# A depthwise convolution that takes taps two to seven over all channels at once, with x laid out as channels 3r+k, in a fused convolution and SiLU layer

## The chip, the core and the metric

The kernel runs on one core of a Trainium2 chip. The core has a matrix engine (TensorE), a vector engine (VectorE), a scalar engine (ScalarE), GpSimd, and SyncE, which here issues the transfers (DMAs). Each engine runs its own instructions in their order and waits on semaphores for the others. The metric is the device time of one execution in microseconds (us), less being better. Three runs of the kernel before took 2359.43, 2358.92 and 2358.91 us, median 2358.92.

## The reference

x has 8 sequences of 4096 tokens with 192 channels. A causal convolution over 7 tokens is followed by a two-layer network with SiLU, on 32768 tokens:

```python
w = np.exp(weight - np.max(weight, axis=-1, keepdims=True))
w = w / (np.sum(w, axis=-1, keepdims=True) + 1e-09)      # weight: (8 heads, 7 taps)
out = np.einsum('hk,bskhg->bshg', w, x_unf)               # head = 24 adjacent channels, same 7 taps
h = x @ w_in                                              # (32768, 192) @ (192, 2048)
g = h * (1.0 / (1.0 + np.exp(-h)))
return (g @ w_out).astype(np.float32)                     # (2048, 192)
```

All 24 channels of a head share their seven taps.

## The kernel before

**Tiling.** The tokens are worked through in 32 blocks of 1024. A block is two halves of 512 tokens. Channels lie in partitions: 64 of the 192 channels in 64 partitions, once for each half of the block, so that 128 partitions hold a third (k = 0, 1, 2) of the channels of all 1024 tokens, 512 elements long. In the kernel before, third k is channels 64k to 64k+63. x comes in with 12 transfers per block (`load`, L171), in runs of 32 channels (128 bytes), tokens in partitions; VectorE turns 32 x 32 pieces round (`turn_in`, L461, one instruction per third), the last six tokens of the half before are put in front (`halo_in`), and then `conv` (L489) does tap one on ScalarE and taps two to seven on VectorE, a multiply-and-add each, separately for each third: 3 + 18 instructions. The result is copied by 11 transfers (`spread`, L505) into the tile `dup`, for both row halves of TensorE, and `win` (L519) makes five sums and differences of it.

**The two matmuls.** Both use bilinear schemes that save products. Going up, sums of weight blocks (made once, by GpSimd) are multiplied with `win` or `dup`: 15 products (`product`, L611) for each of five groups, each 64 x 128 weights against 512 columns, on the upper or the lower row half of TensorE; two of them run side by side. A float32 matmul is two passes in the profile. A group's products go into three PSUM banks in chains: a product is added to a bank, the bank is read, the next product is added to the same bank. Which bank it is stands in `CHAIN_BANKS`; six more matmuls per block (`plain`, L635) use `PLAIN_BANKS`. Between products, ScalarE copies a bank out (`u`, L674), VectorE adds it to another bank (`X`, `a`, `b`, L668), and ScalarE takes SiLU (`S` L686, `SL` L691) into the tiles `g`. Going down, VectorE makes four differences `t` of `g` tiles for each of four j (`sum_g`, L694; three buffers `t`, shared with the output tile), and `out_slot` (L711, L741) multiplies: 48 slots per block of four matmuls side by side with 32 columns of weights each, into six banks. `merge` (L782) adds these up (M, y, x, z), `turn_out` transposes back and `store_out` writes.

**The order.** It is written out by hand in two lists and pinned. `START` opens the first blocks; `PLAN`, 129 slots divided by `|`, is run once per block. Slots are numbered from 0 here. A token names a step: P9.4 is product 9 of group 4; L.nk a plain matmul; u, X, a, b, S with a group after the point; t.ji difference i of j; Di.je a down slot; w.i a step of `win`; ld a load; i.k a transposition; v.ki tap i of third k (i from 0); sp.k a spread; o and st output. A `-` ahead means the block before, `+` the block after, and so i, v, sp and w work one block further ahead than the P beside them. Every engine gets its own part of the list in this order. In the list before, P and L stand in slots 50 to 128 and in 0 and 1, D in slots 2 to 49.

**The opening.** The softmax of the taps is spread to partitions by one matmul with a 0/1 matrix `hot` (L448); block 0's convolution is done on TensorE for two thirds, with diagonal matrices (L1001 to L1017), and its up and down products are plain. Meanwhile VectorE rounds the weights (`rounded`, L283).

Of the kernel before, what the change touches and what calls it, by code (L numbers as in the profile page):

```python
# [9 lines left out]
F32 = mybir.dt.float32  # L10
# [7 lines left out]
def kernel(  # L18
# [45 lines left out]
    assert D == NK * R == H * grp and NK == NP == 3 and S % TT == 0 and DFF == 4 * P * NJ  # L64
# [17 lines left out]
        "P5.0 | -P8.3 -S3.2 -sp.2 v.00 -t.01 | -D1.31 -S2.3 -S5.2 | -D1.01 -a0.2 -S1.3 =st.2 "  # L82
        "-a0.3 -S1.1 | -D1.11 -b5.3 -S0.2 | -D0.00 -S5.4 v.22 -sp.0 -S4.3 | -D2.01 -t.03 "
        "-S5.1 -S1.2 | -D0.20 =st.0 -t.02 -S0.3 | -D1.21 -S5.3 v.01 | -D2.00 v.11 | -D5.01 "
        "+ld.0 | -D0.30 v.02 | -D3.00 -t.10 | -D0.01 +ld.1 v.23 | -D0.31 v.24 | -D4.00 -t.11 "
        "+ld.2 | -D3.01 -w.0 | -D4.01 | -D0.11 -t.13 | -D2.11 -w.1 | -D5.00 | -D4.11 -t.12 | "
        "-D5.11 | -D2.10 -t.20 | -D4.10 -t.21 | -D5.10 | -D0.21 | -D0.10 -t.23 | -D3.11 "
        "-z1.0 v.25 u5.0 | -D4.20 v.03 | -D1.10 -t.22 | -D3.10 | -D4.21 -t.30 | -D1.20 v.12 "
        "| -D2.20 -t.31 | -D2.21 | -D1.30 -t.32 | -D3.21 -t.33 | -D5.20 | -D2.31 v.04 | "
        "-D1.00 v.26 | -D4.31 -w.2 | -D2.30 v.05 | -D5.30 -y2.0 | -D3.20 v.06 -y1.0 -M1.0 | "  # L90
        "-D3.31 v.13 | -D3.30 -M2.0 | -D5.31 v.14 -x0.0 | -D4.30 -y0.0 -M3.0 | -D5.21 -x1.0 "
        "| P2.0 | L.00 -M4.0 -x2.1 -w.3 | L.01 | P5.4 u4.0 -w.4 | L.02 | P6.0 u5.4 v.15 | "
        "P3.0 | P2.4 SL.0 v.16 u2.0 | L.12 -x2.3 X2.0 | L.11 -x2.2 u4.4 | L.10 -M5.0 | P9.0 "
        "| P1.0 +i.0 SL.2 SL.1 | P13.0 | P6.4 +i.1 -x2.0 u0.0 X4.0 | P3.4 | P5.1 u2.4 +i.2 "
        "S2.0 | P7.0 | P0.0 -M6.0 +ha.0 X2.4 | P12.0 | P11.0 u1.0 a5.0 u5.1 | P9.4 | P1.4 "
        "b1.0 S4.0 | P13.4 | P4.0 u0.4 X4.4 -w.5 | P10.0 | P2.1 a1.0 | P0.4 | P7.4 u4.1 b5.0 "
        "S2.4 | P11.4 | P8.0 -o.1 u1.4 a5.4 | P6.1 | P12.4 S4.4 a0.0 | P14.4 | P14.0 -M7.0 "
        "u2.1 S0.0 b1.4 | P4.4 | P3.1 S3.4 +v.10 | P10.4 | P1.1 X2.1 S3.0 a1.4 | P5.2 | P9.1 "
        "u0.1 | P0.1 | P13.1 u5.2 X4.1 | P2.2 b5.4 | P8.4 -o.3 | P7.1 | P5.3 u4.2 a0.4 -st.3 "
        "u1.1 | P6.2 | P12.1 S2.1 a5.1 u5.3 | P11.1 | P3.2 -st.1 b1.1 u2.2 S5.0 | P4.1 | "  # L100
        "P10.1 X2.2 S4.1 sp.1 | P2.3 S1.0 | P9.2 a1.1 -o.0 | P1.2 | P8.1 u4.3 X4.2 | P6.3 | "
        "P13.2 u0.2 a0.1 +v.20 | P11.2 b5.1 | P7.2 u2.3 -o.2 S2.2 | P0.2 | P3.3 S4.2 a5.2 | "
        "P1.3 | P12.2 u1.2 X2.3 | P4.2 u0.3 | P9.3 b1.2 S0.4 | P14.1 | P10.2 S1.4 X4.3 | "
        "P0.3 S3.1 | P7.3 b5.2 | P11.3 u1.3 a1.2 | P12.3 S0.1 a5.3 | P14.3 | P13.3 +v.21 | "
        "P4.3 S3.3 b1.3 | P8.2 a1.3 | P10.3 | P14.2 t.00"
# [1005 lines left out]
```

## Time and profile before

| | us |
|---|---|
| median of three runs | 2358.92 |
| the profiled execution | 2359.21 |
| its span, first to last instruction | 2357.4 |
| TensorE busy | 2349.2 |
| VectorE busy | 2110.6 |
| ScalarE busy | 1179.4 |
| taps two to seven, L498 (564 of 128x512, mean 755 ns) | 415.4 |
| transpositions of x, L464 (96 of 128x512, mean 687 ns) | 63.7 |

The page has the busy time of each engine; as instructions of one engine overlap a little, the busy time of a group can be more than the time it holds the engine up. A matmul of 512 columns is shown with 0.59 us, from its issue to the end of its results, while the next one on the same part of the array follows earlier. The timeline lists instructions by start, each with its length; a bracket is the idle time before it and what ended it. The chain is the sequence of work that ended last, followed back from the end. The granted TensorE clock was 0.999.

### The profile page before, as it was taken

How to read it: one execution, taken by the hardware profiler on the slowest of the kernel's cores; microseconds unless marked ns; L12 is line 12 of the kernel's file. 1: busy time of each engine (PE TensorE's matmuls, PEld its weight loads, DVE VectorE, ACT ScalarE, POOL GpSimd, SP SyncE). 2: the span in 40 equal slices, each digit the busy share in tenths (PEclk: the TensorE clock that was granted, in tenths of full speed). 3: DMA queues.
4: the chain of work that ended last, by engine and by line, in shares of the span. 5: the costliest groups of instructions: out<-in, count | busy, mean ns of one | idle time of the engine just before them, and what ended most of it. 6: DMA issues, size and time to landing. Idle time of an engine off the chain costs nothing.

```text
span 2357.4 us, 43991 instructions
## 1 busy us (share of the span) xinstructions
PE 2349.2 (100%) x17630; PEld 1043.8 (44%) x17630; DVE 2110.6 (90%) x2877; ACT 1179.4 (50%) x2275; POOL 105.7 (4%) x168
## 2 busy tenths in 40 slices
PE   9999999999999999999999999999999999999998
PEld 4344443444444444444444444444444444444444
DVE  8999989899899999998998999999999989899867
ACT  5345644456544465444564445654446644456443
POOL 4910000000000000000000000000000000000000
PEclk9999999999999999999999999999999999999999
DMA  7232111222112221222221122212222112222111
GB/s 158 51 66 52 37 35 35 52 53 47 26 33 52 53 53 29 38 40 52 53 43 28 35 53 52 52 23 36 48 52 52 36 32 37 52 53 39 21 20 28
DMA packets 451245, 106.56 MB, mean 45 GB/s; under 512 B 423584, under 2 KB 428704, under 8 KB 451040
## 3 DMA queue, kind: packets, MB, share of 16 engines
q1 hardware_dynamic: 447392, 101.78, 23.7%
q8 instruction: 138, 2.26, 0.4%
q0 software_dynamic: 448, 1.58, 0.3%
q10 hardware_dynamic: 3200, 0.39, 0.1%
q14 instruction: 67, 0.55, 0.1%
HBM read 31.46 MB, written 25.17 MB: 24 GB/s over the span
## 4 chain that ended last, share of the span: by engine, by line
PE 99%; DVE 1%; ACT 0%; issue 0%; ACTq 0%; DVEq 0%
PE ps L741 47%; PE ps L625 45%; PE ps L642 2%; PE ps L762 2%; PE ps L570 2%; PE ps L1010 1%; PE ps L422 0%; DVE t L709 0%; DVE g L668 0%; DVE cmb L819 0%; DVE cmb L162 0%; ACT u L162 0%; ACT yx L804 0%; DVE osb L162 0%; DVE win L532 0%
## 5 line engine op out<-in xcount | busy, mean ns | idle before, releaser
L741 PE MATMUL ps<-g,wo 128*32 128x512 f32 x2976 | 691.9, 592 | 0.0
L625 PE MATMUL ps<-win,wr 64*128 64x512 f32 x1550 | 691.3, 595 | 0.0
L625 PE MATMUL ps<-win,ws 64*128 64x512 f32 x1550 | 674.3, 603 | 0.6 <-ACT u L674 0.6
L674 ACT COPY u<-ps 128x512 f32<-128x512 f32 x775 | 445.8, 589 | 184.6 <-PE ps L625 158.0
L741 PE MATMUL ps<-t,wo 128*32 128x512 f32 (+2 forms) x4528 | 536.6, 446 | 0.5 <-DVE t L709 0.5
L741 PE MATMUL ps<-t,wx 128*32 128x512 f32 x2976 | 495.7, 592 | 0.0
L625 PE MATMUL ps<-dup,wr 64*128 64x512 f32 x868 | 423.8, 590 | 0.0
L498 DVE SCALAR_TENSOR_TENSOR nat<-xt,taps,nat 128x512 f32<-128x512 f32 x564 | 415.4, 755 | 5.6 <-ACT nat L495 2.0
L709 DVE TENSOR_TENSOR t<-g 128x1024 f32<-128x1024 f32 x248 | 299.9, 1220 | 61.1 <-PE ps L741 41.0
L709 DVE TENSOR_TENSOR t<-g,t 128x1024 f32<-128x1024 f32 x248 | 302.7, 1221 | 30.0 <-PE ps L741 24.7
L625 PEld LDWEIGHTS ps<-win,wr 64*128 64x128 f32 x1550 | 261.4, 186 | 148.3 <-issue 62.4
L686 ACT ACTIVATE g<-ps 128x512 f32<-128x512 f32 x465 | 275.4, 602 | 83.8 <-PE ps L625 78.0
L668 DVE TENSOR_TENSOR g<-u,ps 128x512 f32<-128x512 f32 x465 | 305.7, 673 | 10.1 <-PE ps L625 1.4
L741 PEld LDWEIGHTS ps<-t,wo 128*32 128x32 f32 x4528 | 185.4, 110 | 274.2 <-issue 270.6
L625 PEld LDWEIGHTS ps<-win,ws 64*128 64x128 f32 x1550 | 242.6, 185 | 144.8 <-issue 49.5
L625 PE MATMUL ps<-dup,ws 64*128 64x512 f32 x682 | 280.9, 602 | 0.0
L668 DVE TENSOR_TENSOR ps<-u,ps 128x512 f32<-128x512 f32 x310 | 214.5, 692 | 69.8 <-PE ps L625 64.0
L686 ACT ACTIVATE g<-g 128x512 f32<-128x512 f32 x465 | 268.4, 633 | 15.3 <-DVE g L668 15.3
L804 ACT COPY yx<-ps 32x512 f32<-32x512 f32 x150 | 84.2, 579 | 380.0 <-PE ps L741 377.6
L741 PE MATMUL ps<-g,wx 128*32 128x512 f32 x1488 | 246.0, 594 | 0.0
L741 PEld LDWEIGHTS ps<-g,wo 128*32 128x32 f32 x2976 | 170.1, 110 | 112.5 <-issue 103.9
L807 ACT COPY cmb<-ps 96x512 f32<-96x512 f32 x30 | 17.5, 583 | 403.8 <-PE ps L741 403.8
(90 smaller groups left out, 1849.2 us busy)
## 6 DMA issues: line engine op xcount, KB each, us to landing
dup<-nat SPq DMA_DIRECT2D x345, 128.0 KB, 2.3
nat<-in_x_dram SPq DMA_DIRECT2D x382, 64.0 KB, 2.4
out_dram<-osb SPq DMA_DIRECT2D x376, 64.0 KB, 2.0
raw<-in_moe_w_out_dram SPq DMA_DIRECT2D x8, 384.0 KB, 3.6
raw<-in_moe_w_in_dram SPq DMA_DIRECT2D x12, 192.0 KB, 4.5
ws<-wr POOLq DMA_DIRECT2D x8, 192.0 KB, 5.0
raw<-in_moe_w_in_dram SPq DMA_DIRECT2D x6, 128.0 KB, 3.0
xt<-xt SPq DMA_DIRECT2D x31, 4.5 KB, 1.9
```

The costliest lines, as they stand in the source:

```text
L498: nc.vector.scalar_tensor_tensor(out=dst, in0=src, scalar=tap, in1=dst, op0=ALU.mult, op1=ALU.add)
L570: nc.tensor.matmul(hs[a, n, e], rows(wr[j], e)[:, a, k, :], rows(d, e)[:, n, k, :], start=k == 0, stop=k == NK - 1,)
L625: nc.tensor.matmul(to[:, cols], raw(g, *LEFT[e][r], e), rhs[:, cols], start=first, stop=True, skip_group_check=True,)
L642: nc.tensor.matmul(banks[PLAIN_BANKS[n and 1 + e]][:, cols], rows(wr[j] if own == e else ws[j], e)[:, a, k, :], rows(dups[b], e)[:, SLOT[e ...
L668: pin(nc.vector.tensor_tensor(out_, u, v, op=op))
L674: pin(nc.scalar.copy(us[b, g, o][:, cols], t1[:, cols]))
L686: pin(nc.scalar.activation(h, src, AF.Silu))
L709: pin(nc.vector.tensor_tensor(t[i // 2][:, i % 2, :], u, v, op=ALU.subtract))
L741: nc.tensor.matmul(accs[b][at][SQ * q : SQ * q + SQ, to], lhs[:, e, SQ * k : SQ * k + SQ], rhs[:, e, ts(q, TB // 4) if i == 5 else to], st ...
L762: nc.tensor.matmul(banks[DOWN_BANKS[k]][R * n : R * n + R, :], wo[j][:, a, e, R * k : R * k + R], gs[b, j, a][:, n, e, :], start=j == 0 an ...
L804: pin(nc.scalar.copy(to, acc[3 * (name[0] == "x") + k][n:P, :]))
L1010: nc.tensor.matmul(by_pe[k][n], rows(diag, n)[:, k, i, :], rows(xts[0], n)[:, k, i : i + TB], start=i == 0, stop=i == K - 1,)
```

## The change

Third k becomes the channels 3r+k, in partition r. A head's 24 channels are then eight partitions in every third, so a partition has the same seven taps in all three thirds; `taps` shrinks from three columns per tap to one, and the matrix that spreads them from 96 rows to 8. Taps two to seven become one VectorE operation each over 128 x 3 x 512 elements (v.31 to v.36; the first tap stays with ScalarE, three operations). x is loaded in runs of 96 channels (384 bytes) with four transfers per block; the transposition of third k reads every third element of the token's row. The rows of w_in are taken as (r k). In the opening, block 0's x is loaded whole ahead of the first transposition, and one set of seven diagonal matrices replaces two. `PLAIN_BANKS` is (7, 4, 3) instead of (7, 7, 3). Both lists are new: in `PLAN` ten D slots (119 to 128) now stand between the last products and P5.0, -P8.3 of the next turn, which are followed by the other 38 (2 to 39); P and L stand in 40 to 118. The list `START` is left out below.

```diff
     PLAN = (
-        "P5.0 | -P8.3 -S3.2 -sp.2 v.00 -t.01 | -D1.31 -S2.3 -S5.2 | -D1.01 -a0.2 -S1.3 =st.2 "
-        "-a0.3 -S1.1 | -D1.11 -b5.3 -S0.2 | -D0.00 -S5.4 v.22 -sp.0 -S4.3 | -D2.01 -t.03 "
-        "-S5.1 -S1.2 | -D0.20 =st.0 -t.02 -S0.3 | -D1.21 -S5.3 v.01 | -D2.00 v.11 | -D5.01 "
-        "+ld.0 | -D0.30 v.02 | -D3.00 -t.10 | -D0.01 +ld.1 v.23 | -D0.31 v.24 | -D4.00 -t.11 "
-        "+ld.2 | -D3.01 -w.0 | -D4.01 | -D0.11 -t.13 | -D2.11 -w.1 | -D5.00 | -D4.11 -t.12 | "
-        "-D5.11 | -D2.10 -t.20 | -D4.10 -t.21 | -D5.10 | -D0.21 | -D0.10 -t.23 | -D3.11 "
-        "-z1.0 v.25 u5.0 | -D4.20 v.03 | -D1.10 -t.22 | -D3.10 | -D4.21 -t.30 | -D1.20 v.12 "
-        "| -D2.20 -t.31 | -D2.21 | -D1.30 -t.32 | -D3.21 -t.33 | -D5.20 | -D2.31 v.04 | "
-        "-D1.00 v.26 | -D4.31 -w.2 | -D2.30 v.05 | -D5.30 -y2.0 | -D3.20 v.06 -y1.0 -M1.0 | "
-        "-D3.31 v.13 | -D3.30 -M2.0 | -D5.31 v.14 -x0.0 | -D4.30 -y0.0 -M3.0 | -D5.21 -x1.0 "
-        "| P2.0 | L.00 -M4.0 -x2.1 -w.3 | L.01 | P5.4 u4.0 -w.4 | L.02 | P6.0 u5.4 v.15 | "
-        "P3.0 | P2.4 SL.0 v.16 u2.0 | L.12 -x2.3 X2.0 | L.11 -x2.2 u4.4 | L.10 -M5.0 | P9.0 "
-        "| P1.0 +i.0 SL.2 SL.1 | P13.0 | P6.4 +i.1 -x2.0 u0.0 X4.0 | P3.4 | P5.1 u2.4 +i.2 "
-        "S2.0 | P7.0 | P0.0 -M6.0 +ha.0 X2.4 | P12.0 | P11.0 u1.0 a5.0 u5.1 | P9.4 | P1.4 "
-        "b1.0 S4.0 | P13.4 | P4.0 u0.4 X4.4 -w.5 | P10.0 | P2.1 a1.0 | P0.4 | P7.4 u4.1 b5.0 "
-        "S2.4 | P11.4 | P8.0 -o.1 u1.4 a5.4 | P6.1 | P12.4 S4.4 a0.0 | P14.4 | P14.0 -M7.0 "
-        "u2.1 S0.0 b1.4 | P4.4 | P3.1 S3.4 +v.10 | P10.4 | P1.1 X2.1 S3.0 a1.4 | P5.2 | P9.1 "
-        "u0.1 | P0.1 | P13.1 u5.2 X4.1 | P2.2 b5.4 | P8.4 -o.3 | P7.1 | P5.3 u4.2 a0.4 -st.3 "
-        "u1.1 | P6.2 | P12.1 S2.1 a5.1 u5.3 | P11.1 | P3.2 -st.1 b1.1 u2.2 S5.0 | P4.1 | "
-        "P10.1 X2.2 S4.1 sp.1 | P2.3 S1.0 | P9.2 a1.1 -o.0 | P1.2 | P8.1 u4.3 X4.2 | P6.3 | "
-        "P13.2 u0.2 a0.1 +v.20 | P11.2 b5.1 | P7.2 u2.3 -o.2 S2.2 | P0.2 | P3.3 S4.2 a5.2 | "
-        "P1.3 | P12.2 u1.2 X2.3 | P4.2 u0.3 | P9.3 b1.2 S0.4 | P14.1 | P10.2 S1.4 X4.3 | "
-        "P0.3 S3.1 | P7.3 b5.2 | P11.3 u1.3 a1.2 | P12.3 S0.1 a5.3 | P14.3 | P13.3 +v.21 | "
-        "P4.3 S3.3 b1.3 | P8.2 a1.3 | P10.3 | P14.2 t.00"
+        "+ld.0 P5.0 | -P8.3 +ld.1 | -D2.10 -t.13 | -D3.01 -w.0 | -D5.01 | -D4.11 -t.20 | "
+        "-D2.11 -t.21 | -D1.31 | -D4.10 -w.1 | -D0.20 -t.23 | -D5.11 | -D2.21 -a0.3 | -D5.10 "
+        "v.32 -S0.3 | -D3.10 | -D1.01 -t.22 | -D3.11 | -D0.21 v.33 | -D2.20 | -D0.30 -t.30 | "
+        "-D4.21 -t.31 | -D3.20 | -D4.20 v.34 | -D0.01 | -D1.30 -w.2 | -D0.31 v.35 | -D2.30 | "
+        "-D2.31 -w.3 | -D3.21 -t.33 | -D0.11 -t.32 | -D1.00 -z1.0 -y2.0 v.36 | -D5.20 | "
+        "-D4.31 -y0.0 u5.0 | -D1.21 -w.5 | -D5.31 | -D5.30 | -D3.30 -M1.0 -w.4 | -D4.30 | "
+        "-D5.21 | -D3.31 -x2.1 -x2.0 | -D1.10 -x2.3 -M3.0 -x0.0 -x2.2 -M2.0 -y1.0 | L.00 | "
+        "P2.0 -x1.0 +i.0 | L.10 u4.0 +i.1 | P3.0 | P5.4 -M4.0 | L.01 | P6.0 u5.4 +i.2 | L.11 "
+        "u2.0 | L.02 | P2.4 X2.0 | L.12 -o.1 u4.4 | P9.0 | P1.0 SL.0 -M5.0 -st.1 SL.2 | P6.4 "
+        "| P13.0 u0.0 X4.0 SL.1 | P5.1 | P3.4 u2.4 S2.0 | P0.0 | P7.0 X2.4 | P11.0 | P12.0 "
+        "u1.0 a5.0 u5.1 | P1.4 | P9.4 b1.0 S4.0 | P4.0 | P13.4 u0.4 X4.4 | P10.0 | P2.1 a1.0 "
+        "| P0.4 | P7.4 b5.0 u4.1 | P11.4 | P8.0 u1.4 a5.4 S2.4 -M7.0 | P6.1 | P12.4 S1.0 "
+        "a0.0 | P4.4 | P14.4 u2.1 b1.4 | P3.1 | P14.0 S3.4 a1.4 S4.4 -o.2 | P1.1 | P10.4 "
+        "S5.0 X2.1 -st.2 | P5.2 | P8.4 u0.1 b5.4 | P9.1 | P0.1 a0.4 u5.2 +ha.0 S3.0 | P12.1 "
+        "| P2.2 X4.1 u1.1 -M6.0 | P13.1 | P5.3 u4.2 b1.1 | P7.1 | P6.2 S2.1 -o.0 | P3.2 "
+        "-st.0 | P11.1 a5.1 u2.2 | P10.1 u5.3 | P4.1 X2.2 S0.0 S4.1 | P9.2 | P1.2 b5.1 +v.00 "
+        "a1.1 | P13.2 | P2.3 u0.2 X4.2 S5.1 | P8.1 t.00 | P0.2 S2.2 u4.3 | P7.2 | P11.2 a0.1 "
+        "+v.10 | P12.2 u1.2 | P6.3 a5.2 S1.4 | P3.3 | P14.2 b1.2 u2.3 S4.2 | P10.2 X2.3 | "
+        "P1.3 | P9.3 | P4.2 b5.2 u0.3 | P0.3 | P12.3 X4.3 a1.2 | P11.3 | P7.3 u1.3 -o.3 S3.2 "
+        "| P13.3 | P14.1 b1.3 -st.3 S1.2 a5.3 S0.1 | P8.2 | P14.3 S4.3 t.02 | P4.3 | P10.3 "
+        "sp.1 S3.1 S5.2 t.01 | D0.00 S5.4 S0.4 | D1.20 b5.3 +v.20 sp.0 t.03 S2.3 | D1.11 "
+        "S1.1 | D0.10 a0.2 sp.2 t.10 | D5.00 | D3.00 a1.3 | D2.01 t.11 S1.3 | D4.01 S3.3 "
+        "S0.2 | D2.00 +v.31 S5.3 | D4.00 t.12"
     )
...
     START = (
...
     CHAIN_BANKS = ((0, 1, 7, 1, 0), (2, 3, 2, 3, 2), (4, 4, 4, 4, 4))
+    PLAIN_BANKS = (7, 4, 3)
...
-    def load(b, ks=range(NK)):
+    def load(b, ns=range(2)):
         if b not in nats:
-            nats[b] = nats[b % 2] if b > 1 else xpool.tile([P, NK, TB // SQ, SQ], F32, tag="nat", name="nat", bufs=2)
-        nat = nats[b]
-        for k in ks:
-            for i in range(P // SQ):
-                c = R * k + SQ * (i % 2)
-                queue = nc.scalar if not b and k == 0 and i % 2 == 0 else nc.sync
+            nats[b] = nats[b % 2] if b > 1 else xpool.tile([P, NK, TB], F32, tag="nat", name="nat", bufs=2)
+        flat = nats[b].rearrange("p k t -> p (k t)").rearrange("p (q d) -> p q d", d=HD)
+        for n in ns:
+            for e in range(2):
+                i = 2 * n + e
+                queue = nc.scalar if not b and not e else nc.sync
                 pin(
                     queue.dma_start(
-                        out=nat[SQ * i : SQ * i + SQ, k, :, :],
-                        in_=x_v[2 * b + i // 2][:, :, c : c + SQ],
+                        out=flat[SQ * i : SQ * i + SQ],
+                        in_=x_v[2 * b + n][:, :, HD * e : HD * e + HD],
                     )
                 )
 
...
-    x0 = x.flatten_outer_dims()[TB - pad : TB, :].rearrange("t (k c) -> c k t", k=NK)
+    x0 = x.flatten_outer_dims()[TB - pad : TB, :].rearrange("t (c k) -> c k t", k=NK)
...
-    hot = const.tile([KR, 2, R], F32, name="hot")
-    wown = const.tile([KR, NK, K], F32, name="wown")
+    hot = const.tile([H, 2, R], F32, name="hot")
+    wown = const.tile([H, K], F32, name="wown")
...
+    own = grp // NK
+    for sign, base in ((1, 0), (-1, own - 1)):
+        pool.affine_select(
+            out=hot,
+            in_=hot,
+            compare_op=ALU.is_ge,
+            fill=0.0,
+            base=base,
+            pattern=[[0, 2], [sign, R]],
+            channel_multiplier=-sign * own,
+        )
...
-    in32 = moe_w_in.bitcast(I32).rearrange("(k r) (a m c) -> r k a m c", r=R, a=2, m=NM)
+    in32 = moe_w_in.bitcast(I32).rearrange("(r k) (a m c) -> r k a m c", r=R, a=2, m=NM)
...
-    taps = const.tile([P, NK, K], F32, name="taps")
+    taps = const.tile([P, K], F32, name="taps")
...
-    load(0, (1, 2))
...
-    for k in range(NK):
-
-        vec.tensor_scalar(
-            wown[SQ * k : SQ * k + H, k, :], wexp, scalar1=part_, scalar2=None, op0=ALU.mult
-        )
+    vec.tensor_scalar(wown, wexp, scalar1=part_, scalar2=None, op0=ALU.mult)
...
-                xts[b][:, k, pad : pad + TB], nats[b][:, k, :, :].rearrange("p k c -> p (k c)")
+                xts[b][:, k, pad : pad + TB].rearrange("p (q c) -> p q c", c=SQ),
+                nats[b].rearrange("p k t -> p (k t)").rearrange("p (q c k) -> p k q c", c=SQ, k=NK)[:, k],
...
     def conv(b, k, i):
 
-        src = xts[b][:, k, i : i + TB]
-        dst = nats[b][:, k, :, :].rearrange("p k c -> p (k c)")
-        tap = taps[:, k, i : i + 1]
+        k = slice(None) if k == NK else k
+        src, dst = xts[b][:, k, i : i + TB], nats[b][:, k]
+        tap = taps[:, i : i + 1]
...
-    PLAIN_BANKS = (7, 7, 3)
...
-            pool.tensor_copy(warm, nats[1][:, digits[0], 0, 0:1])
+            pool.tensor_copy(warm, nats[1][:, 0, 0:1])
...
-    diag = gpool.tile([P, NK - 1, K, P], F32, tag="g", name="diag")
+    diag = gpool.tile([P, K, P], F32, tag="g", name="diag")
...
-    def diagonal(k):
+    def diagonal():
         for i in range(K):
-            act.activation(diag[:, k, i, :], one_hot, AF.Copy, scale=taps[:, k, i : i + 1])
+            act.activation(diag[:, i, :], one_hot, AF.Copy, scale=taps[:, i : i + 1])
...
-    diagonal(0)
+    diagonal()
     conv_pe(0)
     round_in(0, 0)
-    diagonal(1)
```

## The prediction

> **What bounds the kernel now.** I read the page first (parts 1, 4, 5), then the chain in order of time, then the timeline of one block in the middle.
>
> Parts 1 and 4 of the page:
>
> ```profile
> PE 2349.2 (100%) x17630; PEld 1043.8 (44%) x17630; DVE 2110.6 (90%) x2877; ACT 1179.4 (50%) x2275; POOL 105.7 (4%) x168
> PE 99%; DVE 1%; ACT 0%; issue 0%; ACTq 0%; DVEq 0%
> ```
>
> TensorE sets the end; nothing that another engine saves counts unless it shortens a wait of TensorE. The chain in order of time gives the beat (start us, us, what; L741 are the D slots, L625 the P products):
>
> ```profile
> 215.58 36.22 PE ps L741 x384
> ...
> 256.88 31.07 PE ps L625 x140
> 287.95 36.22 PE ps L741 x384
> ...
> 329.26 31.07 PE ps L625 x140
> 360.33 36.22 PE ps L741 x384
> ```
>
> One block takes 360.33 - 287.95 = 72.38 us: 36.22 of D and 36.16 of P with the six L entries. What would it take without a wait? In an undisturbed stretch of P the passes follow at 0.429 us (13 passes from 1199.31 to 1204.89), two row halves of the array at once. A product is two passes on one half, so it costs 0.429: 75 products and 6 plain ones make 81 x 0.429 = 34.75 us. The P section therefore loses 36.16 - 34.75 = 1.41 us per block, 2% of the block. D loses about nothing: 40 full slots at 0.86 and 8 short ones at 0.22 make 36.16.
>
> Where the 1.41 lies, from the timeline of TensorE, ScalarE and VectorE (start, us, engine, line, operation; in brackets the idle time before):
>
> ```profile
> 1192.60 0.69 PE L625 MATMUL ps<-win,wr 64*128 64x512 f32 x1
> 1193.13 0.59 PE L625 MATMUL ps<-win,wr 64*128 64x512 f32 x1
> 1193.76 0.59 ACT L674 COPY u<-ps 128x512 f32<-128x512 f32 x1 [0.37 <-PE ps L642]
> 1194.42 0.67 PE L625 MATMUL ps<-win,ws 64*128 64x512 f32 x1
> ...
> 1209.62 0.59 PE L625 MATMUL ps<-dup,wr 64*128 64x512 f32 x1
> 1209.82 0.69 PE L625 MATMUL ps<-win,ws 64*128 64x512 f32 x1
> 1210.35 0.83 PE L625 MATMUL ps<-win,ws 64*128 64x512 f32 x2
> ```
>
> The first four lines are one turn of a PSUM bank: P2.0 writes it, u4.0 copies it out, P6.0 adds into it 1.82 us after P2.0 started. The last three show a pass starting 0.2 us late and the next 0.1: such a turn did not fit. From 1209.62 to the first D at 1228.76 there is work for 42 passes, 18.02 us; it took 19.14, so 1.1 of the 1.41 is lost here, in the second half of the section. The rest is 0.2 at the two changes between P and D and some 0.1 early on.
>
> VectorE, as busy as it looks, has room: instructions follow faster than their durations say.
>
> ```profile
> 1232.22 1.22 DVE L709 TENSOR_TENSOR t<-g,t 128x1024 f32<-128x1024 f32 x1
> 1233.36 1.22 DVE L709 TENSOR_TENSOR t<-g 128x1024 f32<-128x1024 f32 x1
> 1234.49 2.07 DVE L498 SCALAR_TENSOR_TENSOR nat<-xt,taps,nat 128x512 f32<-128x512 f32 x3
> ```
>
> From start to start: a sum t 1.14, a tap (2.07 - 0.75) / 2 = 0.66; chained sums and merges 0.61 and transposes 0.60 to 0.62 likewise. Per block 18 x 0.66 + 16 x 1.14 + 48 x 0.61 + 7 transposes x 0.61 = 63.7 us of 72.4.
>
> **What the Trainium skill says.** "TensorEngine Tiling (Array Packing)", Key Properties: changing the tiling mode drains TensorE. The trace agrees: in the opening list an isolated pair of products stands between D slots; the D passes before it end at about 162.66, the pair starts at 162.77 and D goes on at 163.83, so 1.17 us for 0.86 of work: 0.31 for going there and back. "VectorE: DVE Perf Modes", The TRN2 errata: a fixed cost per instruction, for fp32 tensor_tensor (N + 151) / 0.96 ns; at 512 that is 691, the trace has 690 (win<-win,dup). "SBUF — State Buffer", Door 1: 16-byte lines, two hits per line wanted, a stride of up to 4 fp32 said to be free. The new transposes read at a stride of 3 fp32, 1.33 hits a line: the page can be read both ways, and no row here has that stride (8 bytes, in the weight rounding, costs nothing visible: 628 against 667 ns). "DMA: Bandwidth & Descriptors", Why small descriptors are slow: fixed cost per packet; x in runs of 384 instead of 128 bytes is a third of the packets. DMA is at 24% and ends no wait of note.
>
> **The change, part by part.**
>
> Taps: 18 VectorE operations of 512 become 6 of 1536. Slope from 512 to 1024 elements in the rows above: (1.14 - 0.60) / 512 = 1.05 ns per element, so one costs 0.66 + 1.08 = 1.74 us from start to start, between 1.6 (element rate alone) and 1.98 (nothing saved). Saving 3 x 0.66 - 1.74 = 0.24, times 6 = 1.5 us of VectorE per block. It is off TensorE's path: worth nothing by itself. What counts is where the work stands: all six are now among D slots, while the old list had v.15, v.16 among P.
>
> VectorE's load by section, counted from the lists: before, P 32.3 and D 31.3 us; after, P 29.0 and D 33.1, for 34.8 and 36.2 of TensorE. So the section that loses time gets 3.3 us of room, and D is filled to 91%.
>
> Is D then late? The tightest place in the new list is t.13, wanted by D4.11 three slots later. VectorE from the first D slot on: 1.0 to 1.5 left over, then b5.3 0.61, t.03 1.14, a0.2 0.61, t.10 1.14, a1.3 0.61, t.11 1.14, v.31 1.74, t.12 1.14, t.13 1.14, together 10.3 to 10.8. TensorE until D4.11: eleven full slots 9.46, two short ones 0.44, the pair P5.0 and P8.3 1.17, together 11.07. It holds by 0.3 to 0.8 us; with 1.98 for v.31 still by 0.1 to 0.6. I count 0, with 0.3 as the bad end.
>
> The isolated pair: P5.0 and -P8.3 stood at the end of P; now ten D slots come ahead of them. Two more changes of mode per block: +0.31 us, nothing hides it.
>
> Bank turns: I counted, in each list, the TensorE time between a write to a bank and the next write to it where a read stands between. A turn needs 0.86 (own two passes) + 0.2 to the reader's start + 0.59 (copy) or 0.69 (sum) + 0.05, so 1.7 to 1.8, more if the reader's queue is busy. Turns with 1.72 or less: 15 in the old list, 12 of them among slots 86 to 123 where the loss was found; 8 in the new one, seven of them between slots 84 and 109. The shortest, 1.29, stands once among P in each (P1.1 to P0.1; P1.3 to P0.3). Overlapping turns share a stall, so I scale: 8 / 15 of 1.1 us = 0.6, and with a less busy VectorE ahead of X, a and b 0.5 to 0.7. Early in P L.12 no longer waits for the SiLU of its bank (bank 4 now): 0.1. Relief 0.6; high end 1.1; low end -0.2: v.00 and v.10 (0.72 each) and the SiLUs crowd ScalarE around slots 92 to 105, and behind them wait u0.2, u1.2 and u2.3, for which P0.2, P14.2 and P1.3 wait.
>
> Transposes, three per block: 0.60 if the stride is free, 1.1 if it halves the rate. Slots 41 to 46 have nothing else on VectorE but M4; at 1.1 each the queue is 1.3 us late there and P9.0 (waiting for X2.0) about 0.4. I take 0, range 0 to 0.5.
>
> Start: the first transpose now needs all of x's first block (4 transfers of 192 KB) where it needed 4 of 64 KB. It ran at 5.60, right behind the taps copy; 192 KB transfers of weights land in 4.5 us against 2.4 to 2.5 for x, so I expect it 0.5 to 1.4 us later; +0.9. One scaling of the weights instead of three saves 0.5 there, all behind that load. The second set of diagonals saves ScalarE 2.1 us, hidden by 12 us of matmuls. SP issues 4 loads instead of 12 per block, 40 slots before the transposes: 0. New waits: v.00 writes a tile that all three transposes read, but they stand 48 slots (some 20 us) earlier. The 11 spreads now stand together at slots 118 to 122, with the next loads behind them on SP: 11 x 0.61 us of issue (four took 2.43) + 2.3 to landing = 9.0 us, and w.0, the first to need them all, comes after t.13, at 10.3 or later. P5.0 needs only the first four. 0.
>
> Sum per block: -0.6 + 0.31 = -0.3 us; 29 blocks run by this list: -8.5. Start +0.9. The opening list and the end I take as equal (either way 2 us). The profiled execution took 2359.21 us (span 2357.4 and 1.8 around it), 0.3 above the median of 2358.92. 2359.2 - 8.5 + 0.9 = 2351.6, less 0.3: 2351.5.
>
> **Rivals.**
> - *Relief and pair cancel* (0.20): the stalls fall by 0.2 to 0.4 only. For it: ScalarE's copies, not VectorE, end the worst turns. 2354.5 to 2363.5.
> - *The pair is paid and the stalls stay* (0.20), slower: 0.31 x 29 + 0.9 = +9.9, 2369. It is so if the loss after slot 84 is still over 1.0 us. For it: the new list packs seven short turns into 26 slots.
> - *The stride is not free* (0.13), slower: at half rate 0.4 to 0.5 x 29 = 13 on top of the forecast, 2365; decides from about 0.9 us per transpose. At a third of the rate VectorE is 3 us late in slots 46 to 56: some 1.5 us per block, 2395. Against it: the 8-byte reads.
> - *The merged tap is no cheaper* (within the forecast): 1.98 eats the saving, D4.11 still has its operand; within 2 us.
>
> **How the numbers follow.** Forecast, faster, 0.47: 2338 to 2354. A kernel whose runs lie within 0.5 us resolves about 0.2% (4.7 us). Faster is below 2354.2, slower above 2363.6: 0.47, 0.20, 0.33. For 8 in 10: down to the whole loss regained (1.1 - 0.31 per block: 2337) less the 2 us of the opening list, up to the paid pair and a half-rate stride together (2369 and some 9); the third-rate stride (0.04) is left out, and some 0.1 for what I have not listed: 2335 to 2378. The forecast's own range is 2338 to 2354.
>
> **What would show it.** A row of taps 128x1536 at 1.8 us x186, or so; P passes at 0.429 up to slot 84 and a loss of about 0.6 after it; an L625 piece of about 1.1 us between two L741 pieces in every block of the chain; period near 72.1. Transposes at 0.69 mean; at 1.2 the stride counts. Wrong if TensorE waits for t in D, or if P still takes 36.2 less the pair's 0.86.

## The result

The kernel after takes 2373.07 us (median, 2372.49 to 2374.15), the kernel before 2358.98 beside it: ratio 1.006, 95% interval 1.0042 to 1.0077. It is slower by 14 us; I had forecast 2351.5.

From the page of the profile after, parts 1 and 4:

```profile
PE 2359.6 (99%) x17630; PEld 1022.7 (43%) x17630; DVE 2069.0 (87%) x2502; ACT 1176.6 (50%) x2268; POOL 153.0 (6%) x164
...
PE 98%; DVE 1%; POOL 0%; DMA 0%; SPq 0%; issue 0%; ACT 0%; DVEq 0%; ACTq 0%
```

VectorE saved 41.6 us, and TensorE still sets the end. The chain in order of time (L731 are the D slots, L615 the P products, L632 the L entries):

```profile
1235.98 8.08 PE ps L731 x80
1244.06 1.06 PE ps L615 x4
1245.12 28.27 PE ps L731 x304
1273.40 0.62 PE ps L632
...
1278.77 29.93 PE ps L615 x136
1308.70 8.08 PE ps L731 x80
```

The period is 1308.70 - 1235.98 = 72.72 us, 72.71 as a mean; before it was 72.38. Over 29 steady blocks this is 9.8 us (with the means unrounded, 72.712 and 72.375). The first matmul of the way up starts at 21.9 us instead of 18.6: 3.3. The end after the last steady block takes 1.4 more. Together 14.5, the difference of the two spans (2371.9 - 2357.4).

The block divides as follows. D and the pair take 8.08 + 1.06 + 28.27 = 37.41 where 36.22 + 0.86 stood before: +0.33. The P section without the pair goes from 1273.40 to 1308.70, 35.30 us for 73 products and six plain ones, 79 x 0.429 = 33.89 without a wait: it loses 1.41 us. That is the loss of before to the hundredth, by chance: its parts differ, as the next paragraphs show. So the pair is paid, and in sum nothing of the relief arrived.

VectorE's rows answer to the forecast (groups of instructions with shapes apart: count | busy us, mean ns | idle before):

```profile
L489 DVE SCALAR_TENSOR_TENSOR nat<-xt,taps,nat 128x1536 f32<-128x1536 f32 x186 | 337.8, 1816 | 1.1 <-ACT nat L486 0.8
...
L454 DVE STREAM_TRANSPOSE xt<-nat 128x512 f32<-128x512 f32 x96 | 80.5, 865 | 3.0 <-DMA nat<-in_x_dram 3.0
```

And the timeline of VectorE:

```profile
1252.42 1.81 DVE L489 SCALAR_TENSOR_TENSOR nat<-xt,taps,nat 128x1536 f32<-128x1536 f32 x1
1254.15 1.22 DVE L699 TENSOR_TENSOR t<-g 128x1024 f32<-128x1024 f32 x1
```

A merged tap takes 1.73 us from start to start (forecast 1.74). A transposition takes 865 ns; it took 687.

**Where in P the loss stands.** For each product I took the start of its first pass from the timeline and subtracted the passes issued before it in the section, 0.2145 us each (both row halves counted, a 256-column pass as half). What remains is the lag; where it rises, TensorE waited. Increments in us, one block in the middle (a place has the name of the product at which the rise is read; the one that waited can stand beside it):

```
before: up to P1.0 0.27 | P13.1 .13  P12.1 .08  P13.2 .09  P14.1 .12  P7.3 .09  P11.3 .11  P10.3 .20  P14.2 .11 | first D .21 | 1.41
after:  up to P1.0 0.51 | P9.2+P1.2 .27  P10.2+P1.3 .26  P12.3+P11.3+P7.3 .27                                  | first D .10 | 1.41
```

The late part, with the first D, did fall, 1.14 to 0.90; the early part, up to P1.0, rose by the same 0.24.

Three steps instead of eight does not mean fewer waits, for in this sum a wait of one row half can hide behind the other half. A product that waited can be told in the timeline by its first pass, which lasts longer. P0.2 of the kernel after starts only 0.01 us later than its half is free; its first pass (the first line) lasts 0.69 us instead of 0.59, and its second (the third line) follows after 0.54 us, while the other half (the second and fourth lines) goes on at 0.43:

```profile
1298.58 0.69 PE L615 MATMUL ps<-win,ws 64*128 64x512 f32 x1
1298.99 0.59 PE L615 MATMUL ps<-win,wr 64*128 64x512 f32 x1
1299.12 0.59 PE L615 MATMUL ps<-win,ws 64*128 64x512 f32 x1
1299.42 0.59 PE L615 MATMUL ps<-win,wr 64*128 64x512 f32 x1
```

So a wait costs its own length and some 0.1 us more, however short it is: of the .27 at P9.2, .16 is the wait and .10 comes behind it. In the second half of P ten passes of the block before last 0.64 us or more, and eleven of the block after. The waits became shorter, not fewer.

### The profile page after: what moved, and what is told of

The parts are those of the page before. It is cut to its first block, busy times and chain, and to the rows that moved or that the text cites. A ratio compares the mean times of both kernels' runs of the same rounds, so it can differ in the third digit from the quotient of the medians.

```text
span 2371.9 us, 43339 instructions
## 1 busy us (share of the span) xinstructions
PE 2359.6 (99%) x17630; PEld 1022.7 (43%) x17630; DVE 2069.0 (87%) x2502; ACT 1176.6 (50%) x2268; POOL 153.0 (6%) x164
## 4 chain that ended last, share of the span: by engine, by line
PE 98%; DVE 1%; POOL 0%; DMA 0%; SPq 0%; issue 0%; ACT 0%; DVEq 0%; ACTq 0%
PE ps L731 47%; PE ps L615 43%; PE ps L632 4%; PE ps L752 2%; PE ps L561 2%; PE ps L1000 1%; POOL ws L161 0%; POOL wr L161 0%; DMA nat<-in_x_dram 0%; DVE g L658 0%; DMA dup<-nat 0%; SPq L506 0%; DVE t L699 0%; DVE xt L454 0%; SPq L828 0%
## 5 line engine op out<-in xcount | busy, mean ns | idle before, releaser
L615 PE MATMUL ps<-win,wr 64*128 64x512 f32 x1550 | 714.3, 598 | 0.0
L731 PE MATMUL ps<-g,wo 128*32 128x512 f32 x2976 | 706.8, 593 | 0.0
L615 PE MATMUL ps<-win,ws 64*128 64x512 f32 x1550 | 626.2, 606 | 0.0
L731 PE MATMUL ps<-t,wo 128*32 128x512 f32 (+2 forms) x4528 | 543.9, 446 | 1.2 <-DVE g L658 0.7
L731 PE MATMUL ps<-t,wx 128*32 128x512 f32 x2976 | 485.9, 593 | 0.2 <-DVE g L658 0.2
L676 ACT ACTIVATE g<-g 128x512 f32<-128x512 f32 x465 | 281.6, 637 | 353.8 <-DVE g L658 353.8
L615 PE MATMUL ps<-dup,wr 64*128 64x512 f32 x868 | 415.7, 600 | 1.3 <-POOL wr L161 1.3
L489 DVE SCALAR_TENSOR_TENSOR nat<-xt,taps,nat 128x1536 f32<-128x1536 f32 (+1 forms) x192 | 342.3, 1783 | 4.4 <-ACT nat L486 3.9
L658 DVE TENSOR_TENSOR g<-u,ps 128x512 f32<-128x512 f32 x465 | 316.7, 682 | 17.9 <-PE ps L615 7.9
L615 PE MATMUL ps<-dup,ws 64*128 64x512 f32 x682 | 322.4, 595 | 0.0
L615 PEld LDWEIGHTS ps<-win,wr 64*128 64x128 f32 x1550 | 270.7, 186 | 116.0 <-issue 70.6
L615 PEld LDWEIGHTS ps<-win,ws 64*128 64x128 f32 x1550 | 222.0, 185 | 152.3 <-DVE ps L658 55.5
L731 PEld LDWEIGHTS ps<-t,wo 128*32 128x32 f32 x4528 | 178.8, 110 | 206.4 <-issue 192.1
L731 PE MATMUL ps<-g,wx 128*32 128x512 f32 x1488 | 250.6, 592 | 0.0
L731 PEld LDWEIGHTS ps<-g,wo 128*32 128x32 f32 x2976 | 167.7, 110 | 152.5 <-issue 130.3
L731 PEld LDWEIGHTS ps<-t,wx 128*32 128x32 f32 x2976 | 118.1, 110 | 247.1 <-issue 246.5
```

Source lines behind the costliest of these rows:

```text
L489: nc.vector.scalar_tensor_tensor(out=dst, in0=src, scalar=tap, in1=dst, op0=ALU.mult, op1=ALU.add)
L615: nc.tensor.matmul(to[:, cols], raw(g, *LEFT[e][r], e), rhs[:, cols], start=first, stop=True, skip_group_check=True,)
L658: pin(nc.vector.tensor_tensor(out_, u, v, op=op))
L676: pin(nc.scalar.activation(h, src, AF.Silu))
L731: nc.tensor.matmul(accs[b][at][SQ * q : SQ * q + SQ, to], lhs[:, e, SQ * k : SQ * k + SQ], rhs[:, e, ts(q, TB // 4) if i == 5 else to], st ...
```

## The experiments

**The pair.** First, the pair moved in the kernel before:

```diff
-        "P5.0 | -P8.3 -S3.2 -sp.2 v.00 -t.01 | -D1.31 -S2.3 -S5.2 | -D1.01 -a0.2 -S1.3 =st.2 "
-        "-a0.3 -S1.1 | -D1.11 -b5.3 -S0.2 | -D0.00 ...
+        "-S3.2 -sp.2 v.00 -t.01 -D1.31 -S2.3 -S5.2 | -D1.01 -a0.2 -S1.3 =st.2 -S1.1 | -D1.11 "
+        "-b5.3 -S0.2 | P5.0 | -P8.3 -a0.3 | -D0.00 ...
```

> Kernel before, with its list changed in one thing: P5.0 and P8.3 no longer close the P section but stand behind three down slots (D1.31, D1.01, D1.11). Nothing else of the new kernel is in it. Theory (the isolated pair costs 0.33 us per block and explains the whole steady loss): 29 x 0.33 = +9.5 us, so about 2368.5 us, the period 72.38 -> about 72.7, and a chain piece of about 1.06 us of P between two pieces of D in every block. Rival (the change of mode is hidden, the loss in the new kernel comes from its order of P and its first taps in P): 2359 +- 1 us, period 72.38.

Measured 2392.70 us, ratio 1.0142 (1.0125 to 1.0159), period 73.51: +1.13, far more than either expected. The chain tells why:

```profile
1317.27 0.02 issue
1317.29 0.60 ACT g L686
1317.90 0.04 issue
1317.94 2.78 PE ps L741 x24
1320.72 1.06 PE ps L625 x4
```

D now begins 0.86 us earlier and waits about 0.7 us for a SiLU that the pair had covered (ahead of the first D the lag rises by 0.89 instead of 0.21). The pair itself costs (1.06 - 0.86) + (2.78 + 33.64 - 36.22) = 0.40. Two effects in one run; so I measured the change of mode alone. P5.0 is made twice, which changes nothing in the result: beside itself (the control), or deep in D (isolated). Q5.0 is the second one.

```diff
-        "P5.0 | -P8.3 ...
+        "P5.0 | Q5.0 | -P8.3 ...
```

```diff
-        ... | -D2.11 -w.1 | -D5.00 | ...
+        ... | -D2.11 -w.1 | Q5.0 | -D5.00 | ...
```

> Kernel before, with product P5.0 made twice per block (the second overwrites the first with the same numbers), both next to each other at the end of P, so without another change of mode. Control for the next run. Two passes on one row half: +0.86 us per block, 29 x 0.86 = +24.9 us, 2384 us, period 73.24. Less than that if the pair's place before D hides waits for SiLU or for a bank; more if VectorE's work in D falls late, which it should not, since D starts later.

> The same second P5.0, now alone behind the down slot D2.11, eighteen slots into D: the same work plus going to the P mode and back, and nothing that P or the SiLUs give to D is moved. Theory (a change of mode and back costs about 0.33 us on TensorE's path): 0.33 x 29 = 9.5 us more than the control, about 2393.5 us, period 73.57. Rival (in the two earlier runs the pair cost what it did through waits for SiLU and banks, the change itself is small): within 2 us of the control.

Control: 2379.88 us, ratio 1.0086 (1.0071 to 1.0102), period 73.11. Isolated: 2393.67, ratio 1.0146 (1.013 to 1.0161), period 73.57. The chain of the isolated one:

```profile
1245.48 14.95 PE ps L741 x144
1260.43 1.05 PE ps L625 x2
1261.48 21.41 PE ps L741 x240
...
1287.98 31.07 PE ps L625 x140
```

P is untouched (31.07). D takes 14.95 + 21.41 = 36.36 for 36.22, the lone product 1.05 for 0.86: 0.33 us for going there and back. The two runs differ by 13.8 us, not 9.5, because the control gained 0.13 per block (+0.73 instead of +0.86): its second P5.0 covers part of the wait ahead of the first D (0.09 there instead of 0.21). The Trainium skill, "TensorEngine Tiling (Array Packing)", Key Properties, says that a change of the tiling mode drains TensorE. The trace agrees that a change costs time; the page gives no price, and here it is 0.33 us for both ways, with one product or two.

Then the other way round, the pair put back in front of D in the kernel after:

```diff
-        "+ld.0 P5.0 | -P8.3 +ld.1 | -D2.10 ...
+        "+ld.0 +ld.1 -D2.10 ...
...
-        ... | P4.3 | P10.3 sp.1 S3.1 S5.2 t.01 | D0.00 ...
+        ... | P4.3 a1.3 t.02 | P10.3 S3.1 S5.2 t.01 | +P5.0 | P8.3 | D0.00 ...
```

> Kernel after, with P5.0 and P8.3 moved ahead of the ten down slots, directly behind P10.3, so that P is one piece again (sp.1, a1.3, S3.3 and t.02 moved with it). Theory (the pair is the whole steady loss): -0.33 x 29 = -9.5 us, about 2363.5 us, period about 72.38. Rival (the pair hides nothing, or the drain is paid anyway at the one change): 2373 us. Between the two, some 2367: then the two products add a bank wait at their new place.

Measured 2413.49 us, ratio 1.023 (1.0214 to 1.0245), period 74.11. Not 9.5 us faster but 40 slower. Timeline at the end of P:

```profile
1254.81 1.12 PE L616 MATMUL ps<-dup,wr 64*128 64x512 f32 x2
1254.97 0.69 DVE L659 TENSOR_TENSOR g<-u,ps 128x512 f32<-128x512 f32 x1 [1.41 <-PE ps L616]
...
1255.71 1.12 PE L616 MATMUL ps<-win,wr 64*128 64x512 f32 x2
```

P8.3 adds into the bank that a1.3 reads after P4.3, three slots earlier. Here it cannot stand beside P5.0 (1254.81) but starts after the sum, 0.9 us later. The rest, 0.7 in D and the later first D, I did not follow further. In the new order the ten D slots ahead of the pair are therefore not a plain loss: they fill the bank turn of P8.3, which here costs 0.47 of the 1.40 us that the block is longer. In the old order P8.2, P10.3, P14.2 and P5.0 stand between P4.3 and P8.3.

**Are the readers too busy?** My relief rested on a less busy VectorE, with a crowd of first taps on ScalarE as the low end. So these were taken away:

```diff
-        ... | P1.2 b5.1 +v.00 a1.1 | ... | P11.2 a0.1 +v.10 | ... | D1.20 b5.3 +v.20 sp.0 ...
+        ... | P1.2 b5.1 a1.1 | ... | P11.2 a0.1 | ... | D1.11 S1.1 +v.00 | D0.10 ... +v.10 | D5.00 +v.20 ...
```

> Kernel after, with the three first taps of ScalarE (0.73 us each) taken out of the P section and put behind the down slots D1.11, D0.10 and D5.00. Theory A (the missing relief: the new list packs v.00 and v.10 in front of the copies u0.2, u1.2 and u2.3, and they keep the late loss in P at 0.9 us): the loss in P falls by 0.3 to 0.5 us per block, 2359 to 2364 us, period 72.2 to 72.4. Theory B (the late loss belongs to the short bank turns themselves, at whatever load of ScalarE): 2373 +- 1.5 us, period 72.7.

Measured 2373.98 us, ratio 1.0062 (1.0047 to 1.0077), period 72.71: Theory B. With t.00 moved too (`P8.1 t.00` to `t.00 P14.3`):

> Kernel after, with the first taps of ScalarE behind three down slots as in the run before this one, and t.00 of VectorE (1.22 us) moved from slot 97 to slot 116, so that neither engine has anything but bank reads, SiLUs and two output steps in slots 88 to 112. Theory (turns are bound by their own length, not by how busy their readers are, which is why the relief I forecast from a less busy VectorE did not come): 2373 +- 2 us, late loss in P 0.8 to 1.0 us. Rival (t.00 in front of a0.1 and the sums behind it makes the loss): 2364 or less.

Measured 2387.93 us, ratio 1.0121 (1.0106 to 1.0136). The total misses, since VectorE, with t.00 in its new place, works without a pause from 1314.79 on, is late with a t, and D waits for it:

```profile
1318.79 1.22 DVE t L699
...
1320.05 4.72 PE ps L731 x48
```

But the lags in P are those of the kernel after to 0.01 in all but two blocks (.27, .25, .27 late, 1.40 in all). Emptier readers do not shorten these waits.

**Are the turns themselves too long?** Then a shorter read must help, in the same order:

```diff
-            cols = columns(half)
+            cols = columns(0 if b > 2 and 0 < g < 4 else half)
             pin(nc.scalar.copy(us[b, g, o][:, cols], t1[:, cols]))
```

and the same columns for the sums X, so that half of the tokens are left out of them.

> Kernel after, where the copies u and the sums X of groups 1 to 3 (the later part of P) read half the columns of their bank; the other half of h is left out of the sums, so the output is not the reference's. This shortens what stands between two writes of a bank by about 0.29 us (copy 0.59) and 0.34 us (sum 0.69) and changes no order. Theory (the loss in P is in bank turns of 1.7 to 1.8 us that are shorter in the order than in time): of the 0.9 us of loss late in P at least 0.6 goes, 29 x 0.6 = 17 us, 2350 to 2357 us, P section 34.6 us without the pair or less. Rival (the late loss has another cause: order on TensorE, operands, SiLU): 2370 us or more.

Measured 2363.23 us, ratio 1.0016 (1.0009 to 1.0023), period 72.36; in the chain P takes

```profile
1273.35 29.57 PE ps L615 x136
```

instead of 29.93. The lag shows it place by place: P9.2+P1.2 falls from .27 to 0, P12.3 to P7.3 from .27 to .01, and P10.2+P1.3 stays at .26: there the sum b1.2, still of full width, stands between P12.2 and P10.2 in their bank. So two of the three late places are turns of a bank behind u and X. The gain is 0.36, not the 0.6 expected, and the time lies between the theory and its rival: b1.2 was not shortened, and the first D now waits .28 instead of .10.

**What the early part waits for.** The timeline after, at the change from D to P:

```profile
1273.33 0.69 PE L615 MATMUL ps<-win,wr 64*128 64x512 f32 x1
1273.47 0.68 DVE L809 TENSOR_TENSOR cmb<-cmb,ps 96x512 f32<-96x512 f32 x1 [0.18 <-PE ps L731]
...
1274.20 1.06 ACT L794 COPY yx<-ps 32x512 f32<-32x512 f32 x2
...
1274.84 0.69 PE L615 MATMUL ps<-dup,wr 64*128 64x512 f32 x1
...
1275.29 1.29 ACT L664 COPY u<-ps 128x512 f32<-128x512 f32 x2
...
1275.92 0.69 PE L615 MATMUL ps<-win,ws 64*128 64x512 f32 x1
```

P2.0 (1273.33) is done at about 1274.5, but u4.0 follows at 1275.29, behind y1.0 and x1.0 (1274.20 and 1274.73), and P6.0 at 1275.92. That turn took 1.82 us before; it takes 2.59. Also, P5.4 (1274.84) waits for bank 1, which the last D slot, D1.10, wrote and M2.0 (1273.47) and y1.0 read. Four edits of the list:

```
yx:    -  ... -M3.0 -x0.0 -x2.2 ... P2.0 -x1.0 ...
       +  ... P6.0 u5.4 +i.2 -x0.0 | ... | L.12 -o.1 u4.4 -x1.0 | ...
d1:    -  -D3.30 -M1.0 -w.4 | -D4.30 | -D5.21 | -D3.31 -x2.1 -x2.0 | -D1.10 -x2.3 -M3.0 -x0.0 -x2.2 -M2.0 -y1.0
       +  -D1.10 | -D3.30 -M1.0 -w.4 -M2.0 -y1.0 | -D4.30 | -D5.21 | -D3.31 -x2.1 -x2.0 -x2.3 -x2.2 -M3.0 -x0.0
d1yx:  both
d1x1:  d1, and of yx only x1.0
```

> Kernel after, with two of ScalarE's copies at the change from D to P moved back: x0.0 from slot 39 to behind u5.4 (slot 46), x1.0 from slot 41 to behind u4.4 (slot 50). Theory (five output copies in a row at the change delay u4.0 to 1275.29, 0.7 us after P2.0 is done, and through it P6.0, u2.0, X2.0 and P9.0; in the list before two of them stood behind u4.0): the early part of P, from its first pass to P9.0, falls from 5.12 to between 4.75 and 4.95 us, 29 x 0.15 to 0.35 = 4 to 10 us, about 2366 us. Rival (the early loss is in L.10, L.11, L.12 and their two halves, or X2.0 waits for the transposes): 2372 us or more.

> Kernel after, with the last five down slots in another order: D1.10 from the end to ahead of D3.30 (it needs no t), and the merges with them: M2.0 and y1.0 behind D3.30, M3.0 and x0.0 behind D3.31. Theory (what holds up early P is bank 1: D1.10 writes it last of all D slots, M2.0 and then y1.0 read it until 1274.73, and P5.4, the first product into bank 1, starts only at 1274.84; P6.0 behind it on its row half, u2.0, X2.0 and P9.0 follow): P5.4 starts right behind the plain matmul ahead of it, the early part of P falls from 5.12 to 4.75 to 4.95 us, 29 x 0.15 to 0.35 = 4 to 10 us, 2363 to 2369 us. Rival (the way over P2.0, u4.0 and P6.0 is as long as that over bank 1): early part 5.0 to 5.1, 2370 to 2373 us.

> Kernel after with both edits of the early part at once: D1.10 with M2.0, y1.0 and M3.0 earlier, and x0.0 and x1.0 behind u5.4 and u4.4. Theory (P6.0 has two ways to it of the same length, over bank 1 and P5.4, and over ScalarE's copies and u4.0; each edit alone cleared one and left the other, so neither gained): u4.0 starts within 0.2 us of the end of P2.0, P5.4 right behind the plain matmul, the early part of P falls from 5.12 to 4.7 to 4.9 us, 29 x 0.2 to 0.4 = 6 to 12 us, 2361 to 2367 us. Rival (a third way, X2.0 or the plain matmuls' own turns, is as long again): early part above 5.0, 2370 us or more.

> As the kernel with both early edits, but x0.0 stays ahead of u4.0; only x1.0 is moved, behind u4.4. Theory (the third way is x0.0 itself: behind u5.4 it holds up u2.0 by 0.3 us, and X2.0, which writes the bank that x0.0 reads, and P9.0 wait; ahead of u4.0 it costs nothing, since P6.0 waits for P5.4 on its row half anyhow): u2.0 starts at the end of P6.0, P9.0 some 0.3 us earlier than in the run before this one, the early part of P 4.75 to 4.85 us, 29 x 0.3 = 9 us less than the kernel after, 2362 to 2365 us. Rival (a fourth way): 2369 us or more.

| | us | ratio (95%) | period | lag up to P1.0 | lag of P in all |
|---|---|---|---|---|---|
| after | 2373.07 | 1.006 (1.0042-1.0077) | 72.71 | .51 | 1.41 |
| yx | 2377.29 | 1.0077 (1.0062-1.0092) | 72.82 | .62 | 1.52 |
| d1 | 2377.35 | 1.0076 (1.0058-1.0094) | 72.81 | .60 | 1.51 |
| d1yx | 2372.22 | 1.0055 (1.004-1.007) | 72.66 | .46 | 1.35 |
| d1x1 | 2371.78 | 1.0053 (1.0038-1.0068) | 72.65 | .11 | 1.35 |

Each theory failed in its time; for yx, d1yx and d1x1 the rival's time holds, and d1 lies above both. The rows show how. yx clears the way over u4.0 and leaves that over bank 1, and x0.0 in its new place (1278.45 there) stands in the way of u2.0, which starts at 1279.05. d1 clears bank 1 (P5.4 no longer waits), and ScalarE's copies hold up u4.0:

```profile
1277.06 1.18 ACT L794 COPY yx<-ps 32x512 f32<-32x512 f32 x2 [0.52 <-DVE cmb L809]
...
1278.26 1.07 ACT L664 COPY u<-ps 128x512 f32<-128x512 f32 x2
```

P2.0 had started there at 1276.21. With both edits P6.0 follows without a wait, and X2.0 behind u2.0, which stands behind x0.0, holds up P9.0. d1x1 clears that as well: up to P1.0 no wait is left but the 0.11 of the first passes. And yet the block is only 0.06 us shorter, because new waits stand right behind: P3.4 .07, P0.1 .13, P7.1 .14, then the same three late places. In that run u0.0 starts 6.62 us after P2.0 (6.33 after it in the kernel after), behind x1.0 in its new place:

```profile
1277.76 0.58 ACT L794 COPY yx<-ps 32x512 f32<-32x512 f32 x1
```

So TensorE came earlier and its readers did not. That the place of x1.0 is the whole of it is argued, not shown; x1.0 behind u2.0, where ScalarE is idle for 0.70 us, was not tried.

**The layout and the merged taps without the new order.** The code of the kernel after with the old lists, the merged taps put among the D slots (first run) or into VectorE's idle times (second):

```
first:  -  v.22 ... v.01 ... v.11 ...     +  v.31 to v.36 in slots 9, 14, 28, 36, 42, 47
second: -  v.22 ... v.01 ... v.11 ...     +  v.31 behind t.02, v.32 w.0, v.33 t.22, v.34 t.31, v.35 w.2, v.36 P2.4
```

> The layout, the loads, the transposes and the merged taps of the kernel after, run by the lists and plain banks of the kernel before (the six merged taps stand among the D slots 9 to 47). Theory (layout and merged taps are worth nothing on TensorE's path, and cost 3.3 us once in the opening): about 2362 us, period 72.38 +- 0.05. Rival 1 (less VectorE work in P relieves the bank turns, which the new list then throws away): below 2357, period 72.2 or less. Rival 2 (the transposes at a stride of 12 bytes, 0.18 us longer each, delay X2.0 early in P): 2364 or more, period 72.45 or more.

> The layout, loads, transposes and merged taps of the kernel after, its opening list, but in the 29 blocks the order of the kernel before (and its plain banks), so without an isolated pair; the merged taps stand where VectorE waited for a t buffer in the earlier run of this kind: v.31 behind t.02, v.32 behind w.0, v.33 behind t.22, v.34 behind t.31, v.35 behind w.2, v.36 in P behind P2.4. Theory (layout and merging are worth nothing on TensorE's path and cost 3.3 us in the opening, if VectorE's order lets every t and M come in time): 2360 to 2364 us, period 72.35 to 72.45. Rival (1.74 us pieces on VectorE fit the old order nowhere; the earlier run's 73.5 was no matter of place): 2375 or more, with D over 36.5 us.

In the first, the opening list has a load of x ahead of the last taps of the block whose tile it overwrites, so the output is not the reference's; the steady list is whole. Measured 2400.26 us, ratio 1.0173 (1.0158 to 1.0188), D 36.95. The second: 2379.49, ratio 1.0087 (1.0071 to 1.0102), D 36.22 and period 72.96. So D was a matter of place; the second run has the time of its rival and the D of its theory, and neither holds. What is left is in P, and in both runs at the same products: P7.0 and P0.0 wait .22 and .18, P9.4 and P1.4 .23, where the kernel before has nothing (the second has .16 more at P9.0, behind v.36). The timeline of the first run:

```profile
1222.39 1.02 PE L616 MATMUL ps<-win,ws 64*128 64x512 f32 x4
...
1222.78 1.64 DVE L455 STREAM_TRANSPOSE xt<-nat 128x512 f32<-128x512 f32 x2
...
1224.33 0.67 DVE L659 TENSOR_TENSOR ps<-u,ps 128x512 f32<-128x512 f32 x1
...
1225.06 0.69 PE L616 MATMUL ps<-win,wr 64*128 64x512 f32 x1
```

X4.0 stands behind two transpositions and starts 1.94 us after P9.0; in the kernel before it was 1.48. P7.0 starts when X4.0 is done, and P9.4 (1227.00) when X2.4 (1226.25) is, which stands behind the third transposition. In the old order the slower transpositions are on TensorE's path and cost some 0.4 us per block (.45 and .41). The new list has them in slots 41, 42 and 46, ahead of every X, where they cost nothing. The Trainium skill, "SBUF — State Buffer", Door 1, can be read as letting a stride of up to 4 fp32 go free; the trace does not agree: at a stride of 3 they take 865 ns instead of 687.

**The opening.**

```diff
-    turn_in(0, 0)
-
     vec.memset(xts[0][R:P, 1:NK, 0:pad], 0.0)
     for k in range(1, NK):
         halo(k, nc.gpsimd)
+    turn_in(0, 0)
```

> Kernel after, with the clearing of the first tokens of thirds 1 and 2 and their two small transfers ahead of the first transposition in the opening. Theory (half of the 3.3 us that the opening lost is these transfers, which wait for VectorE behind the transposition, which waits for the load of x; the tapped matmuls wait for them, 13.9 us instead of 12.2): -1.7 us once, 2371.3 us, period unchanged at 72.71. Rival (the opening is bound by the weights' way in, and what is gained there is lost behind it): within 0.5 us of 2373.

Measured 2371.25 us, ratio 1.0053 (1.0036 to 1.007), period 72.71: 1.8 us, as expected. In the timeline after, the transposition, the diagonal matmuls and the two transfers:

```profile
7.21 0.86 DVE L454 STREAM_TRANSPOSE xt<-nat 128x512 f32<-128x512 f32 x1 [1.86 <-DMA nat<-in_x_dram]
...
8.22 13.87 PE L1000 MATMUL ps<-xt,diag 64*128 64x512 f32 x56 [2.01 <-DVE xt L161]
...
8.51 1.48 POOL L194 DMA_DIRECT2D xt<-in_x_dram  x2 [6.12 <-DVE xt L161]
```

and with the edit:

```profile
6.08 1.48 POOL L194 DMA_DIRECT2D xt<-in_x_dram  x2 [3.68 <-DVE xt L161]
...
8.23 12.29 PE L1000 MATMUL ps<-xt,diag 64*128 64x512 f32 x56 [1.07 <-DVE xt L454]
```

So of the 3.3 us, 1.6 are the load of x (the transposition at 7.21, formerly 5.60) and 1.6 the two small transfers, which the late transposition held back, since VectorE clears their place behind it.

**Together.** The opening's edit with yx gave 2374.73, with d1 2374.31, with d1yx 2370.25, with d1x1:

> The edit of the run before this one and the opening's transfers ahead of the first transposition: 2 us less than the run before this one, 2360 to 2363 by the theory, so level with or just above the kernel before, with the pair's 9.6 us still in it.

Measured 2370.14 us, ratio 1.0049 (1.0032 to 1.0065): 7 to 10 us more than the theory, level with the run with d1yx, and still 11 us above the kernel before. No version beat the kernel before.

## Why the prediction was wrong

- *What bounds the kernel; VectorE's saving worth nothing by itself; D in time.* Right. D with its restart takes 36.35, and t.13 held nothing up.
- *Merged tap 1.74.* Right: 1.73.
- *Pair +0.31, hidden by nothing.* Right: +0.33, by the trace after and by the product isolated in the kernel before. What I did not see is what its place buys: the bank turn of P8.3.
- *Bank turns, relief 0.6.* This is the step that failed. I counted turns of 1.72 us or less, 15 against 8 (late in P 12 against 7), and scaled the loss with the count. The short turns did become fewer, but the products that waited did not: late in P ten before, eleven after, some of them (P12.3, P7.3) outside my count; and each wait, short or long, brings some 0.1 us with it. The late part, the first D included, gave 0.24, not 0.5. The reason that I gave for more, a less busy VectorE, was no reason: emptying the readers changed nothing, shortening their reads did.
- *Early in P, 0.1 of relief.* Wrong in sign: -0.24. I looked at turns inside P, not at those that begin in D: the new list ends D with the slot that writes bank 1, and sets five output copies ahead of u4.0. This took back the whole late gain. It is not all there to be had: with these waits gone (d1x1) the block was only 0.06 us shorter, as others came up behind them.
- *Transposes 0.* Right for this list, not because the stride is free (0.18 us each), but by their place. In the old order they cost 0.4 per block.
- *Opening +0.9.* Mis-sized: +3.3. The load was 1.6 late, where I had 0.5 to 1.4, and I overlooked the two transfers behind the transposition, 1.6 more.
- *Opening list and end equal.* The end took 1.4 us more, inside the 2 allowed.

With the relief at 0 the sum would read 0.33 x 29 + 3.3 + 1.4 = 14.3 us. The measured difference is 14.1. This is the rival "the pair is paid and the stalls stay" (2369), 4 us short, since the opening took 2.4 more than it had and the end 1.4. Its own sign held only in part: the loss late in P is 0.90, where it asked for over 1.0, and the early part made up the sum.

## What to carry to other kernels

A count of tight places is no price: lay out the lag of the bounding engine instruction by instruction, for each part that runs by itself, and follow each rise to its wait, those that begin in the section before included. Where several waits of about the same length run side by side, removing one shows nothing, and removing all shows the next that lies behind. Before an oddly placed piece is called a loss, ask what wait it covers.

## What the runs showed of the hardware that was new to me

- Going from the D form (128 rows by 32 columns) to the P form and back costs 0.33 us, with one product or two: some 0.19 on the product and 0.14 on D.
- A 128 x 512 fp32 stream transposition that reads every third element takes 865 ns, one that reads adjacent elements 687; size and destination are the same. The stride by itself was not tried in a run. From start to start two of them take 0.78.
- A 512-column pass of P that had to wait on its row half is shown, but for one case, with 0.68 or 0.69 us instead of 0.59, and the second pass of its product starts 0.52 to 0.55 us after it instead of 0.43. In the middle block of the kernels before and after this holds for all fifteen products that were 0.01 to 0.31 us late.
